# A unit's outputs copied by VectorE instead of ScalarE, with 28 score tiles moved from the attention loop to the stage before it

## The chip, the cores and the metric

The kernel runs on one core of one Trainium2 chip. The metric is the device time of one execution in microseconds (us). The kernel before takes 1575.48 us, the median of three runs (1575.44 to 1575.68).

## The reference

The input is 2048 tokens of width 512. They are normalised once, and two branches read the result:

```python
xn = _layernorm(x, axis=-1)
# A: attention, 32 heads of width 16
qkv = (xn @ wqkv).reshape(B, S, 3, H, Dh).transpose(2, 0, 3, 1, 4)
q, k, v = qkv[0], qkv[1], qkv[2]
p = _softmax(jnp.einsum("bhqd,bhkd->bhqk", q, k) * (Dh ** -0.5), axis=-1)
s = jnp.einsum("bhqk,bhkd->bhqd", p, v).transpose(0, 2, 1, 3).reshape(B, S, D) @ wo
# B: a feed-forward of width 1376, and a gate
g = _silu(_gelu(xn @ w1 + b1) @ w2 + b2)
return x + s * g
```

The softmax needs the largest score of each query row before any exponential of that row. The kernel computes every score twice: once only to find the row maxima, and once more, with keys and queries exchanged, to take the exponentials.

## The kernel before

**Units.** The 32 heads are eight groups of four, and the 2048 queries are four chunks of 512. A unit is one group with one chunk: 32 units, numbered u = 4 * group + chunk. A unit has three kinds of work.

- *Score tiles* (`s_mm`, line 171, and `s_max`, line 181). TensorE multiplies 128 queries with 512 keys of one head into one PSUM bank, and VectorE reduces the bank to two maxima a row. A unit has 64 of them, the kernel 2048. The contraction has 48 rows, so two tiles can work side by side on the two halves of TensorE's rows. When the 64th is reduced, `s_end0` (line 234) makes one further reduction of all maxima (line 239), GpSimd (POOL) splits the result into a rounded part and a rest, and `s_end1` (line 256) transposes it and sends it to DRAM, from where it comes back as two more rows of the query tile.
- *Exponential tiles* (`t_one`, line 703). TensorE multiplies 128 keys with 512 queries of one head, two more rows subtracting the maximum, and ScalarE takes the exponential (line 712). A unit has 64.
- *Output steps* (`pv_step`, line 769). Four heads' exponentials of 128 keys are multiplied with the values into one PSUM bank, `pv` (line 775), 16 times a unit. After the 16th, the bank is copied to SBUF (`os`, line 782), and transfers move the copy on (`o_move`, line 792). The pool of `pv` has one buffer, so the next unit's first output matmul waits for that copy.

**The early stage** normalises, projects, and does the feed-forward; its matmuls use one half of TensorE's rows each, in turn (`mm`, line 554, on line 561). Into this stream `fill` (line 538) puts score tiles: a slot is one matmul on each half, and a tile is due after each `ROWS / (4 * LEAD)` slots, alternately on the two halves. `ROWS` is 12 * 80 + 6 * 88 - 10 + 2 * LEAD - 38, with `LEAD` = 144 it is 1728 for 576 tiles. The tiles use two PSUM banks in turn.

**The attention loop** (line 955) has 16 steps a unit, n = 0 to 512. An order of operations is written out for each step: T is an exponential tile, S a score tile on one half, X and Y the two half-width pieces of one more tile, one on each half, and V the output step of the step before. `due(n)` (line 911) says how many score tiles shall be done by step n, and the difference chooses the order: three tiles (`TSXTTSTYV`) until step 491, none (`TTTTV`) after. Score tiles here use three PSUM banks in rotation; X keeps its bank until Y is done. A unit's output copy belongs to the V of step 16 (u + 1). From step 492 on, the first rows of the final product with `wo` fill the place of the score tiles (`w_half`, line 871).

**Key tiles.** The keys of a group lie in one of three places, group modulo three (`KB`, line 42): `kt0`, `kt1`, and two slots of the pool `big`. Groups 3 and later are loaded by POOL's DMA queue into the place of the group three before: group 3 in two halves from step 56 and step 64 (lines 916 to 919), group 4 from step 134, 5 from 198, 6 from 262, 7 from 326. Every twelfth unit takes its tiles in another order, so that a half-loaded key tile can be used (`at_of`, line 167).

What sets the order: each engine works through its instructions in the order of the program; waits between engines are derived from the tiles.

Of the kernel before, what the change touches and what calls it, by code (L numbers as in the profile page):

```python
# [8 lines left out]
F32 = mybir.dt.float32  # L9
F32R = mybir.dt.float32r  # L10
AF = mybir.ActivationFunctionType
# [5 lines left out]
P = 128  # L17
S = 2048
D = 512
H = 32  # L20
DH = 16
KT = D // P
NT = S // P
CH = 512
NCH = S // CH
# [4 lines left out]
EPS = 1e-5  # L30
SCALE = DH ** -0.5
VW = DH + 1
LEAD = 144
NW = 10
EARLY = 4
DONE = 492
FILL0 = 38
HB = 4
W2B = 2
ORDER = {0: "TTTTV", 3: "TSXTTSTYV"}  # L40
HC = CH // 2
KB = 3
XB = 6
BANKS = ("ttvt", "xtmt", "ttvt")

# [2 lines left out]
def fused(ctx: ExitStack, tc: tile.TileContext, x, wqk, wv, wo, w1, b1, w2, b2, out):  # L48
    nc = tc.nc
# [20 lines left out]
    kts, kws, qts, qzs = [], [], [], []  # L70
# [26 lines left out]
    def rows(src, g, which, a, c0, n):  # L97
        r0 = g * P + 64 * which + DH * a
        return src[r0:r0 + 48, c0:c0 + n].rearrange("(p d) s -> d p s", d=DH)[:, 0:3:2, :]

    def load_k(g, pieces=range(6), eng=nc.sync, c0=0, n=S):
        both = kws[g % KB]
        for i in pieces:
            a, b = divmod(i, 3)
            r, cs = slice(64 * a + DH * b, 64 * a + DH * b + DH), slice(c0, c0 + n)
            src = rows((qk_h, qk_h, qk_l)[b], g, 1, a, c0, n)
            if both is not None:
                eng.dma_start(both[r, :, cs].bitcast(F32), src)
            else:
                for p in range(2):  # L110
                    eng.dma_start(kts[g % KB][p][r, cs].bitcast(F32), src[:, p])

    def k_ones(kt):
        for p in range(2):
# [3 lines left out]
    def new_k(pool):  # L118
        both = pool.tile([P, 2, S], F32R, name=f"kt{len(kts)}")
        kws.append(both)  # L120
        kts.append([both[:, p] for p in range(2)])
# [3 lines left out]
    def slot(i, shape, dtype=F32):  # L125
        return big.tile(list(shape), dtype, name=f"slot{i}")

    def q_rows(qs, u, sides=range(2)):
        g, c = divmod(u, NCH)
        for a in sides:  # L130
            for b, src in enumerate((qk_h, qk_l, qk_h)):
                r = 64 * a + DH * b
                nc.sync.dma_start(qs[r:r + DH].bitcast(F32), rows(src, g, 0, a, c * CH, CH))

    def load_qs(u, sides=range(2)):
        if u < NU:
            QS[u] = qzs[u % 2] if u < LEAD // 16 else qss[0][:, u % 2]
            q_rows(QS[u], u, sides)
# [8 lines left out]
    def load_mh(u):  # L147
        assert u in sent
        for a in range(2):
            nc.sync.dma_start(QT[u][64 * a + 48:64 * a + 50].bitcast(F32), mh_d[u, :, a::2, :])  # L150
# [15 lines left out]

    def at_of(job):
        u, st, p = job
        return divmod(st, NCH) if u % (NCH * KB) else divmod(st, NCH)[::-1]

    def s_mm(ps, job, a, c0, k0, w):
        u, st, p = job
        qi, ki = at_of(job)
        if u not in MX:
            MX[u] = qring.tile([P, GH, NCH, NCH, 2], F32, name="mx")
        r = slice(64 * a, 64 * a + 3 * DH)
        k0 += ki * CH
        return nc.tensor.matmul(ps[:, c0:c0 + w], QS[u][r, p, qi * P:(qi + 1) * P],  # L178
                                kts[u // NCH % KB][p][r, k0:k0 + w], start=True, stop=True).ins

    def s_max(ps, job, heads, parts):
        u, p = job[0], job[2]
# [103 lines left out]
    for i in range(nu):  # L286
        pairs.append(ms[2 * i:2 * i + 2])
        if (i + 1) * len(qs) // nu > i * len(qs) // nu:
            g, c = qs[i * len(qs) // nu]
# [4 lines left out]
    for j in range(len(pairs)):  # L294
        for h in range(2):
# [9 lines left out]
            n = 2 if nd < len(parts) and parts[nd][2] and ready - nd > room else 1  # L305
            n = max(n, need - 2 * (left - 1))
            while nd < ready and n > 0:
                c, f, k = parts[nd]
# [33 lines left out]
    keep_v = ctx.enter_context(tc.tile_pool(name="keep_v", bufs=1, side="right"))  # L342
# [170 lines left out]
    keep_r = ctx.enter_context(tc.tile_pool(name="keep_r", bufs=1, side="right"))  # L513
# [21 lines left out]
    ndown = sum(1 for e in plan if e[0] == "down")  # L535
    ROWS = 12 * (4 * VQ + 2 * len(pairs)) + 6 * ndown - 10 + 2 * LEAD - FILL0

    def fill(a):
        due = FILL0 + sum(made) * ROWS // (4 * LEAD)
        if sum(made) < 4 * LEAD and row[a] >= due and (made[0] <= made[1]) == (a == 0):  # L540
            taken()
            if later and later[0][0] <= 0:
                s_end1(later.pop(0)[1])
            s_one(a)
            row[a] += 1
            tick()

    def taken():
        prog["pe"] += 1
        s_when.append(prog["pe"])  # L550
        if len(s_when) > 2:
            prog["seen"] = max(prog["seen"], s_when[-3])
# [142 lines left out]
    def t_tile():  # L695
        turns[0] += 1
        if turns[0] < 5:
            pool = (ps_m, ps_x, ps_a, ps_b)[turns[0] - 1]
        else:
            pool = ps_m if turns[0] % 4 == 1 else ps_t  # L700
        return pool.tile([P, CH], F32, name="pst" if pool is ps_t else "ps")

    def t_one(u, k, p, a):
        g = u // NCH
        if (u, k) not in PT:
            PT[u, k] = slot(3 + len(PN) % 3, (P, GH, CH))
            PN.append(1)
        ps = t_tile()
        r = slice(64 * a, 64 * a + 3 * DH + 2)
        nc.tensor.matmul(ps, kts[g % KB][p][r, k * P:(k + 1) * P],  # L710
                         QT[u][r, p, :], start=True, stop=True)
        nc.scalar.activation(PT[u, k][:, 2 * p + a, :], ps, AF.Exp, scale=SCALE)  # L712

# [33 lines left out]
    kp = ctx.enter_context(tc.tile_pool(name="kp", bufs=1))  # L747
# [2 lines left out]
    qts.append(kp.tile([P, 2, CH], F32R, name="qt1"))  # L750
    load_qt(1)
    load_mh(1)
    wo_h = kp.tile([P, KT, D], F32R, name="wo_h")
    wo_l = kp.tile([P, KT, D], F32R, name="wo_l")

    WR = {}

# [10 lines left out]
    PV, OS, DN, DR = {}, {}, {}, {}  # L768
    def pv_step(u, k):
        g = u // NCH  # L770
        if k == 0:
            PV[u] = ps_v.tile([P, CH], F32, name="pv")
        for j in range(GH):
            h, w = (g * GH + j) * VW, VW if k else 32
            nc.tensor.matmul(PV[u][32 * j:32 * j + w, :], vsb[:, k, h:h + w], PT[u, k][:, j, :],  # L775
                             start=(k == 0), stop=(k == NT - 1))
        del PT[u, k]
        if k == NT - 1:
            OS[u] = wb.tile([P, CH], F32, name="os", bufs=1)
            pv = PV.pop(u)  # L780
            if u < NU - 1:
                nc.scalar.activation(OS[u], pv, AF.Copy)
            else:
                nc.scalar.activation(OS[u][:, :HC], pv[:, :HC], AF.Copy)
                nc.vector.tensor_copy(OS[u][:, HC:], pv[:, HC:])
# [28 lines left out]
    GX, OTS, PW, homes = {}, {}, {}, {}  # L814

    def home(i):
        if i not in homes:
            homes[i] = (slot(i, (P, KT, D)) if i < KB else
                        keep_r.tile([P, 2 * KT, D], F32, name="kt0"))
        return homes[i]  # L820

    def load_gx(t):
        i = 2 * (t % NCH)
        if t < NW and i < 6:
            GX[t] = wb.tile([P, 2, D], F32, name="gx", bufs=3)
        elif t < NT - NCH:
            GX[t] = home(KB)[:, i - 6 * (t < NW):][:, :2]
        else:
            GX[t] = home(1 + i // KT)[:, i % KT:i % KT + 2]
        nc.sync.dma_start(GX[t][:, 0], g_d[t * P:(t + 1) * P, :])  # L830
        nc.sync.dma_start(GX[t][:, 1], x[t * P:(t + 1) * P, :])
# [73 lines left out]
    def at(n, f, *a, pos=3):  # L905
        todo.setdefault((n, pos), []).append((f, a))

    KS = tuple(range(KT))
    L = 16 * NU

    def due(n):
        return min(4 * L, 4 * LEAD + max(0, 3 * n - 1))

    for u in range(NU):
        g, c = divmod(u, NCH)
        if c == 0 and g == KB:
            for i in range(6):
                at(56 + i, load_k, g, (i,), nc.gpsimd, 0, S // 2)
                at(64 + i, load_k, g, (i,), nc.gpsimd, S // 2, S // 2)
        elif c == 0 and g > KB:  # L920
            for i in range(6):
                at(64 * (g - KB + 1) + 6 + i, load_k, g, (i,), nc.gpsimd)
        if u >= 2:
            at(16 * u - 14, load_qt, u)
            need = min(n for n in range(L) if due(n) >= 64 * (u + 1)) + (4 if u < NU - 1 else 2)
            at(max(16 * u - 14, need), load_mh, u)
        if u < NU - 1:
            at(16 * u + 17, o_move, u, pos=0)
            at(16 * u + (25 if u < NU - 2 else 19), o_den, u, pos=0)
            at(16 * u + (31 if u < NU - 2 else 22), o_div, u, nc.gpsimd)  # L930
    T3 = range(NT - NCH, NT)
    late = range(NW, NT)
    for t in range(0, NW, 2):
        n = DONE + 2 * t
# [9 lines left out]
    for i, t in enumerate(late):  # L944
        n = L - 2 * len(late) - 1 + 2 * i
# [2 lines left out]
    for i, t in enumerate(late[:2]):  # L948
        at(L - 2 + i, w_token, t)
    for k in range(KT):  # L950
        at(104 + 16 * k, load_wo, k)
        at(110 + 16 * k, wo_high, k)
        at(114 + 16 * k, wo_low, k)
    jobs.extend(heads[made[0]:])
    for n in range(L + 1):
        ua, ka = divmod(n, 16)
        want = due(n) - due(n - 1)
        i = 0
        for op in ORDER[want] if n > 1 else ("TTTTV", "TTSTSVT")[n]:
            if op in "SXY":  # L960
# [69 lines left out]
```

## Time and profile before

| | us |
|---|---|
| median of three runs | 1575.48 |
| the profiled execution | 1575.59 |
| its span, first to last instruction | 1573.8 |
| from the first score tile to the first output step | 61.4 to 477.3 |
| a unit in the loop | 32.9 |
| last output step | 1549.9 |

TensorE's granted clock is 0.999. In the rows of the profile PE is a TensorE matmul, PEld a TensorE weight load, DVE VectorE, ACT ScalarE, POOL GpSimd and SP the queue that issues most transfers; L775 is line 775. A row of the time line is: start, duration, engine, line, operation, output<-inputs, shapes, count, and in brackets the idle time of the engine before it and what ended that. Weight loads and matmuls overlap, and matmuls overlap one another.

### The profile page before, as it was taken

The numbers are of one execution on the slowest core, as the hardware profiler recorded it, in microseconds if no ns is written. First come the engines' busy times: TensorE is split into PE (matmuls) and PEld (weight loads), VectorE is DVE, ScalarE is ACT, GpSimd is POOL, SyncE is SP. The second block draws the span as 40 slices with busy tenths as digits, with TensorE's granted clock in tenths as the row PEclk, the third lists the DMA queues.
The fourth block names the chain that finished last, engine by engine and source line by source line (L and its number), as shares of the span: only waits on it lengthen the run. The fifth ranks groups of instructions, "written<-read, shape, count | busy, mean of one in ns | idle before, by whom it ended". The sixth has DMA issues, their size and how long they took to land.

```text
span 1573.8 us, 32597 instructions
## 1 busy us (share of the span) xinstructions
PE 1561.6 (99%) x12234; PEld 955.1 (61%) x12234; DVE 1376.2 (87%) x2275; ACT 1254.8 (80%) x2516; POOL 378.0 (24%) x398
## 2 busy tenths in 40 slices
PE   8999999999999999999999999999999999999998
PEld 7899999999995444444444444444444444444455
DVE  7499999999998999999999999999999999999733
ACT  4333433434339999999999999999999999999994
POOL 4135575765641001001100200000010000000144
PEclk9999999999999999999999999999999999999999
DMA  6625442454422114111511411221041111111162
GB/s 208 152 60 141 130 139 99 134 155 123 132 84 76 43 30 72 30 36 36 86 31 31 69 37 36 52 51 29 23 79 30 33 29 31 41 29 23 45 210 100
DMA packets 79486, 116.92 MB, mean 74 GB/s; under 512 B 28868, under 2 KB 29124, under 8 KB 78152
## 3 DMA queue, kind: packets, MB, share of 16 engines
q1 hardware_dynamic: 75580, 101.90, 23.9%
q0 software_dynamic: 3264, 12.35, 4.1%
q8 instruction: 96, 1.57, 0.4%
q10 hardware_dynamic: 484, 0.60, 0.1%
q14 instruction: 62, 0.51, 0.1%
HBM read 84.35 MB, written 25.97 MB: 70 GB/s over the span
## 4 chain that ended last, share of the span: by engine, by line
PE 98%; DVE 1%; issue 0%; DMA 0%; ACT 0%; POOL 0%; DVEq 0%
PE pv L775 33%; PE pst L710 16%; PE ps L710 14%; PE ps L561 13%; PE ps L178 9%; PE pst L561 7%; PE pv L561 2%; PE ps L881 1%; PE ps L438 1%; PE ps L79 1%; PE pst L79 1%; DVE st L399 0%; PE pst L422 0%; DMA xt<-in_x 0%; PE pst L438 0%
## 5 line engine op out<-in xcount | busy, mean ns | idle before, releaser
L184 DVE TENSOR_REDUCE mx<-ps 128x2 f32<-128x512 f32 x2048 | 1299.2, 685 | 129.8 <-PE ps L178 46.7
L712 ACT ACTIVATE slot<-pst 128x512 f32<-128x512 f32 x1533 | 809.5, 616 | 2.1 <-PE ps L710 0.8
L775 PE MATMUL pv<-slot,vsb 128*17 128x512 f32 (+1 forms) x4096 | 539.2, 599 | 0.0
L178 PE MATMUL ps<-kt,slot 48*128 48x512 f32 x1364 | 383.8, 370 | 1.1 <-POOLq L216 1.1
L712 ACT ACTIVATE slot<-ps 128x512 f32<-128x512 f32 x515 | 311.7, 606 | 5.6 <-PE ps L710 3.6
L710 PE MATMUL pst<-qt,kt 50*128 50x512 f32 x1149 | 311.4, 406 | 0.5 <-DVE gt L643 0.3
L710 PEld LDWEIGHTS ps<-qt,kt 50*128 50x128 f32 x387 | 70.7, 183 | 323.6 <-ACT slot L712 322.7
L710 PEld LDWEIGHTS pst<-qt,kt 50*128 50x128 f32 x1149 | 212.1, 185 | 29.7 <-ACT slot L712 11.0
L178 PEld LDWEIGHTS ps<-kt,slot 48*128 48x128 f32 x1364 | 225.4, 184 | 3.1 <-POOLq L216 1.4
L561 PE MATMUL ps<-slot,w1h 64*128 64x512 f32 x1088 | 217.7, 394 | 0.0
L178 PE MATMUL ps<-kt,qz 48*128 48x512 f32 x512 | 213.0, 416 | 0.0
L710 PE MATMUL ps<-qt,kt 50*128 50x512 f32 x387 | 190.8, 495 | 0.0
L178 PE MATMUL ps<-slot,slot 48*128 48x512 f32 x598 | 167.9, 369 | 0.0
L561 PEld LDWEIGHTS ps<-slot,w1h 64*128 64x128 f32 x1088 | 150.4, 186 | 8.6 <-ACT junk L575 2.7
L561 PE MATMUL ps<-slot,w1l 64*128 64x512 f32 x544 | 141.2, 392 | 0.0
L358 POOL TENSOR_TENSOR hl<-hg,hh 128x512 fp32r<-128x512 f32 x76 | 96.8, 1296 | 135.6 <-ACT hh L357 67.2
L575 ACT ACTIVATE junk<-ident_r 1x1 f32<-1x1 f32 x92 | 18.0, 196 | 126.7 <-PE pst L561 118.5
L775 PEld LDWEIGHTS pv<-slot,vsb 128*17 128x17 f32 (+1 forms) x4096 | 69.1, 96 | 81.7 <-issue 23.9
L178 PEld LDWEIGHTS ps<-kt,qz 48*128 48x128 f32 x512 | 93.9, 183 | 16.0 <-DVE mx L184 0.6
L710 PE MATMUL pst<-qt,slot 50*128 50x512 f32 x384 | 102.4, 407 | 0.0
L178 PEld LDWEIGHTS ps<-slot,slot 48*128 48x128 f32 x598 | 98.9, 184 | 0.9
L242 POOL CAST nmh<-nm 128x16 fp32r<-128x16 f32 x32 | 6.3, 197 | 353.6 <-PE pst L710 176.4
(151 smaller groups left out, 1756.7 us busy)
## 6 DMA issues: line engine op xcount, KB each, us to landing
raw<-in_w SPq DMA_DIRECT2D x88, 256.0 KB
qk_h<-hh SPq DMA_DIRECT2D x32, 256.0 KB
qk_l<-hl SPq DMA_DIRECT2D x32, 256.0 KB
qt<-qk_h SPq DMA_DIRECT2D x128, 64.0 KB
slot<-qk_h SPq DMA_DIRECT2D x92, 64.0 KB
g_d<-gt POOLq DMA_DIRECT2D x16, 256.0 KB, 3.3
qt<-qk_l SPq DMA_DIRECT2D x64, 64.0 KB
dn<-den_d SPq DMA_DIRECT2D x128, 32.0 KB
```

The source lines that it names most:

```text
L79: nc.tensor.matmul(ps, lhs[a], rhs[b], start=first and n == 0, stop=last and n == 2)
L178: return nc.tensor.matmul(ps[:, c0:c0 + w], QS[u][r, p, qi * P:(qi + 1) * P], kts[u // NCH % KB][p][r, k0:k0 + w], start=True, stop=True).ins
L184: nc.vector.tensor_reduce(MX[u][:, 2 * p:2 * p + 2, qi, ki][:, heads, parts], ps.rearrange("p (n c) -> p n c", c=HC), axis=AX.X, op=OP.max)
L242: nc.gpsimd.tensor_copy(hl[:, 0], nm)
L358: nc.gpsimd.tensor_sub(hl, raw, hh.bitcast(F32))
L438: nc.tensor.matmul(pq["q", g, c], W1[g][i][:, k * P:(k + 1) * P], (xh, xl)[j][c][:, k], start=n == 0 and k == 0, stop=n == 2 and k == KT - 1)
L561: i = nc.tensor.matmul(ps, lhs[r], rhs[r], start=first, stop=last).ins
L575: i = nc.scalar.activation(junk[:, :1], ident_r[:1, :1].bitcast(F32), AF.Copy).ins
L710: nc.tensor.matmul(ps, kts[g % KB][p][r, k * P:(k + 1) * P], QT[u][r, p, :], start=True, stop=True)
L712: nc.scalar.activation(PT[u, k][:, 2 * p + a, :], ps, AF.Exp, scale=SCALE)
L775: nc.tensor.matmul(PV[u][32 * j:32 * j + w, :], vsb[:, k, h:h + w], PT[u, k][:, j, :], start=(k == 0), stop=(k == NT - 1))
L881: op = nc.tensor.matmul(PW[b][0], OTS[b, k][i][r], (wo_h, wo_l)[j][r, k], start=part == 0 and n == 0, stop=part == 3 and n == 5).ins
```

## The change

1. The copy of a unit's outputs from PSUM (line 782) is made by VectorE instead of ScalarE. The last unit's, which was split between both, stays as it was.
2. `LEAD` is 151: 604 score tiles are made in the early stage, and `ROWS` becomes 1742.
3. `due` gives one tile less from step 50 on and once more every 16 steps, to step 482: those 28 steps have two score tiles and the order `TSTTSTV`. Each is the second step behind the one with a copy. Score tiles still end at step 491.
4. The fourth group (group 3) has its own key tile in the pool `kp`, where `wo_h` and `wo_l` were; these two now use the same tile later. Which group uses which place is written in `KSET`, and the step at which its load begins in `KAT`. Group 3 is loaded whole from step 4, group 4 from step 70, the others as before. The rows of ones of the new tile are written at step 3. Loading and splitting `wo` moves from step 104 to step 266. Only unit 0 takes its tiles in the other order.
5. The late gate tiles that lay in `kt0` lie in `kt1`.

```diff
-LEAD = 144
+LEAD = 151
...
-ORDER = {0: "TTTTV", 3: "TSXTTSTYV"}
+ORDER = {0: "TTTTV", 2: "TSTTSTV", 3: "TSXTTSTYV"}
+LIGHT = 34
 HC = CH // 2
-KB = 3
+KSET = (0, 1, 2, 3, 0, 2, 1, 0)
+KAT = {3: 4, 4: 70, 5: 198, 6: 262, 7: 326}
...
-        return divmod(st, NCH) if u % (NCH * KB) else divmod(st, NCH)[::-1]
+        return divmod(st, NCH) if u else divmod(st, NCH)[::-1]
...
-    wo_h = kp.tile([P, KT, D], F32R, name="wo_h")
-    wo_l = kp.tile([P, KT, D], F32R, name="wo_l")
+    new_k(kp)
+    wo_h, wo_l = [kws[3][:, i].rearrange("p (k d) -> p k d", d=D) for i in range(2)]
...
             if u < NU - 1:
-                nc.scalar.activation(OS[u], pv, AF.Copy)
+                nc.vector.tensor_copy(OS[u], pv)
...
-            homes[i] = (slot(i, (P, KT, D)) if i < KB else
-                        keep_r.tile([P, 2 * KT, D], F32, name="kt0"))
+            homes[i] = (slot(i, (P, KT, D)) if i < 3 else
+                        keep_v.tile([P, 2 * KT, D], F32, name="kt1"))
...
     def due(n):
-        return min(4 * L, 4 * LEAD + max(0, 3 * n - 1))
+        return min(4 * L, 4 * LEAD + max(0, 3 * n - 1 - max(0, (n - LIGHT) // 16)))
...
-        if c == 0 and g == KB:
+        if c == 0 and g in KAT:
+            if g == 3:
+                at(KAT[g] - 1, k_ones, kts[KSET[g]])
             for i in range(6):
-                at(56 + i, load_k, g, (i,), nc.gpsimd, 0, S // 2)
-                at(64 + i, load_k, g, (i,), nc.gpsimd, S // 2, S // 2)
-        elif c == 0 and g > KB:
-            for i in range(6):
-                at(64 * (g - KB + 1) + 6 + i, load_k, g, (i,), nc.gpsimd)
+                at(KAT[g] + i, load_k, g, (i,), nc.gpsimd)
...
-        at(104 + 16 * k, load_wo, k)
-        at(110 + 16 * k, wo_high, k)
-        at(114 + 16 * k, wo_low, k)
+        at(266 + 16 * k, load_wo, k)
+        at(272 + 16 * k, wo_high, k)
+        at(276 + 16 * k, wo_low, k)
```

Wherever a key tile was chosen by `g % KB`, it is now chosen by `KSET[g]`.

More of the change, by code (lines that the diff above doesn't have):

```diff
@@ L101, in load_k @@
     def load_k(g, pieces=range(6), eng=nc.sync, c0=0, n=S):
-        both = kws[g % KB]
+        both = kws[KSET[g]]
         for i in pieces:
@@ L110, in load_k @@
                 for p in range(2):
-                    eng.dma_start(kts[g % KB][p][r, cs].bitcast(F32), src[:, p])
+                    eng.dma_start(kts[KSET[g]][p][r, cs].bitcast(F32), src[:, p])
     def k_ones(kt):
@@ L178, in s_mm @@
         return nc.tensor.matmul(ps[:, c0:c0 + w], QS[u][r, p, qi * P:(qi + 1) * P],
-                                kts[u // NCH % KB][p][r, k0:k0 + w], start=True, stop=True).ins
+                                kts[KSET[u // NCH]][p][r, k0:k0 + w], start=True, stop=True).ins
     def s_max(ps, job, heads, parts):
@@ L709, in t_one @@
         r = slice(64 * a, 64 * a + 3 * DH + 2)
-        nc.tensor.matmul(ps, kts[g % KB][p][r, k * P:(k + 1) * P],
+        nc.tensor.matmul(ps, kts[KSET[g]][p][r, k * P:(k + 1) * P],
                          QT[u][r, p, :], start=True, stop=True)
@@ L826, in load_gx @@
         elif t < NT - NCH:
-            GX[t] = home(KB)[:, i - 6 * (t < NW):][:, :2]
+            GX[t] = home(3)[:, i - 6 * (t < NW):][:, :2]
         else:
```

## The prediction

> **What bounds the kernel now.** The page first, its chain of the work that ended last:
>
> ```profile
> PE 98%; DVE 1%; issue 0%; DMA 0%; ACT 0%; POOL 0%; DVEq 0%
> ```
>
> TensorE (PE) carries 98% of it, which names the engine and not the waits. So I cut the span by stage (PE, PEld, DVE, ACT, POOL busy):
>
> ```profile
> 62.00:477.00 415.00, 414.62 (x3481) 379.80 (x3479) 375.13 (x598) 159.43 (x357) 238.78 (x210) 1.00 0.42 121
> 478.00:1472.00 994.00, 993.89 (x7723) 473.95 (x7720) 921.75 (x1523) 991.18 (x1960) 75.57 (x126) 1.00 0.19 41
> 1472.00:1549.00 77.00, 75.92 (x597) 38.83 (x595) 33.97 (x52) 72.16 (x139) 28.46 (x23) 1.00 0.45 145
> ```
>
> The early stage is TensorE's, with 40 us of VectorE free. The loop has TensorE and ScalarE both full. The chain gives a unit's length, and the time line one end of a unit (start, duration):
>
> ```profile
> 873.00 1.07 PE pv L775 x8
> ...
> 905.91 1.07 PE pv L775 x8
> ```
> ```profile
> 870.90 1.05 PE L775 MATMUL pv<-slot,vsb 128*17 128x512 f32 x8
> ...
> 873.00 0.16 PEld L775 LDWEIGHTS pv<-slot,vsb 128*32 128x32 f32 x8 [0.21 <-ACT os L782]
> ...
> 874.96 0.18 PEld L710 LDWEIGHTS pst<-qt,kt 50*128 50x128 f32 x1 [0.30 <-ACT slot L712]
> ...
> 875.39 1.05 PE L775 MATMUL pv<-slot,vsb 128*17 128x512 f32 x8
> ...
> 877.41 1.05 PE L775 MATMUL pv<-slot,vsb 128*17 128x512 f32 x8
> ```
>
> A unit takes 905.91 - 873.00 = 32.91 us. Its ordinary step is 2.02 to 2.03 (875.39 to 877.41; I use 2.03); the two steps at its end take 2.10 (870.90 to 873.00) and 2.39 (873.00 to 875.39). So a unit holds 0.07 + 0.36 = 0.43 us that come from one thing: ScalarE's copy of the outputs pushes its exponentials back, and weights wait for them.
>
> **The change, part by part.**
>
> *The copy leaves ScalarE.* It goes in 31 units. The last of these copies lies among the steps after 1472, where no score tiles are left and VectorE works 34 of 77 us; it is worth nothing there. 30 x 0.43 = **-12.9 us**.
>
> *The copy on VectorE.* These rows show its queue, and what its lateness would meet:
>
> ```profile
> 871.03 1.28 DVE L184 TENSOR_REDUCE mx<-ps 128x2 f32<-128x512 f32 x2
> ```
> ```profile
> 870.89 1.57 ACT L712 ACTIVATE slot<-pst 128x512 f32<-128x512 f32 x3
> ...
> 872.45 0.41 PE L178 MATMUL ps<-kt,slot 48*128 48x512 f32 x1
> ...
> 872.57 0.43 PE L710 MATMUL pst<-qt,kt 50*128 50x512 f32 x1
> ...
> 876.94 1.89 DVE L184 TENSOR_REDUCE mx<-ps 128x2 f32<-128x512 f32 x3 [0.29 <-PE ps L178]
> ```
>
> Maxima of 0.68 start (1.89 - 0.68) / 2 = 0.60 apart, three a step, 1.81 of 2.03. The step's last maximum starts at 871.63 and ends at 872.31; the copy starts 0.60 behind it, at 872.23, and takes 0.69 if it is like a maximum (no row shows it whole; the nearest reads the same 128x512 from PSUM). It ends at 872.92. The next unit's first output matmul, due at 872.93, waits some 0.04 for it: 30 x 0.04 = **+1.3** (nothing if it is shorter, 3 if 0.1 late).
>
> Behind it the next step's maxima come 0.39 late (872.84 instead of 872.45). The bank of a step's third tile is wanted 0.57 into the next step (the matmul at 872.45; steps begin at 869.86, as a row below shows, and 2.03 later) and is now free at 0.43. Late by 0.39, it would stall that step by 0.25 and some weight loading, 0.3. The step of two score tiles stands there: it does not ask for that bank, and VectorE skips 0.60 of work. So it costs nothing in 28 units; units 0 and 1 have no such step: **+0.6**.
>
> *Light steps.* 28 tiles leave the loop. Each was two half-width matmuls side by side on the two row halves, about 0.12 us. A fourth exponential ends at 870.89 + 1.57 = 872.46, its bank's next matmul starts at 872.57: only 0.11 to spare. Of 0.12, I count 0.08: 28 x 0.08 = **-2.2** (0 to -3.4).
>
> *The unit's closing reduction moves.*
>
> ```profile
> 566.07 1.05 PE L775 MATMUL pv<-slot,vsb 128*17 128x512 f32 x8
> 566.18 0.28 DVE L239 TENSOR_REDUCE nm<-mx 128x16 f32<-128x128 f32 x1
> ...
> 568.26 1.05 PE L775 MATMUL pv<-slot,vsb 128*17 128x512 f32 x8
> ```
>
> Where it falls behind a step's first maximum, it adds 0.2 to VectorE, the third bank comes 0.11 late, and the step takes 2.19: 0.16 lost. That is so in 7 units now and, by the changed order, 13 times: **+1.0**.
>
> *28 more tiles in the early stage.* Each of the rows below is a score tile's matmul or weights (PE, PEld) or its maximum (DVE):
>
> ```profile
> 320.03 0.43 PE L178 MATMUL ps<-kt,qz 48*128 48x512 f32 x1
> ...
> 321.37 0.18 PEld L178 LDWEIGHTS ps<-kt,qz 48*128 48x128 f32 x1
> ...
> 321.47 0.41 PE L178 MATMUL ps<-kt,qz 48*128 48x512 f32 x1
> ...
> 322.21 0.18 PEld L178 LDWEIGHTS ps<-kt,qz 48*128 48x128 f32 x1
> ```
> ```profile
> 320.64 0.68 DVE L184 TENSOR_REDUCE mx<-ps 128x2 f32<-128x512 f32 x1
> ```
> ```profile
> 321.47 0.69 DVE L184 TENSOR_REDUCE mx<-ps 128x2 f32<-128x512 f32 x1
> ```
>
> Two tiles of one bank lie 1728 x 2 / 576 = 6 slots apart (a slot is one matmul on each row half): 320.03 to 321.47, 0.24 a slot. 28 tiles are 14 slots on each half: **+3.4** if nothing waits.
>
> But maxima end at 321.32 and 322.16, and the weights of the tile two behind load at 321.37 and 322.21: 0.05 later both times. They wait for VectorE, and that is hidden only because the matmul starts 0.10 after its weights (321.47). The new spacing is 1742 / 604 = 2.884 slots, which means that 604 x 3 - 1742 = 70 of the spacings are two slots instead of three. Each puts two tiles of one bank 5 slots, 1.20 us, apart. The shortest bank cycle follows from a tile that met an idle array and an idle VectorE:
>
> ```profile
> 869.86 0.50 PE L178 MATMUL ps<-kt,slot 48*128 48x512 f32 x1
> ```
> ```profile
> 870.43 0.69 DVE L184 TENSOR_REDUCE mx<-ps 128x2 f32<-128x512 f32 x1
> ```
>
> 0.57 + 0.69 + 0.05 = 1.31: the bank comes 0.11 late. Bounds: 0 (the matmuls queued on the other half cover it) and 0.24 (the removed slot is lost whole). The nearest row is the step of 2.19 above, where a bank 0.11 late cost 0.16: I take 0.15. 70 x 0.15 = **+10.5**.
>
> The Trainium skill, "TensorEngine Tiling (Array Packing)", section "PSUM Bottleneck", says that tiling speeds up TensorE but not the emptying of PSUM, which may become the limit. The trace agrees (the 0.05 above); if emptying were the whole limit, 28 tiles would cost their full 0.72 each, the second rival's case.
>
> *The fourth group's own key tile.* Its score tiles now begin at step 55, while group 0 is used up to step 64, so it needs a place of its own. Loaded at steps 4 to 9 on POOL's queue, four one-rows at step 3 on SP's, 45 steps (90 us) ahead of use: nothing. Were that place not free, the reductions' rounding on POOL and the query loads on SP would queue behind it; they have most of a unit to spare. The loads of wo move to step 266 and are used at 492: nothing.
>
> **Sum.** -12.9 + 1.3 + 0.6 - 2.2 + 1.0 = -12.2 in the loop, 3.4 + 10.5 = +13.9 before it: **+1.7**. The profiled execution took 1575.6 (1.8 around the span), the median 1575.5: I forecast **1577.2**, no change that can be told. It turns at 70 x = 8.8, that is at 0.126 per short spacing.
>
> **Rivals.**
> 1. *The short spacings are covered* (0.04 each or less). For it: the weights are asked for early, and VectorE idles 40 us there. Against: no lead is left but 0.10. Early stage +6.2: 1569.5. Faster.
> 2. *The early stage runs at VectorE's pace*: a short spacing costs the whole slot, 0.24, beyond the 0.126 at which the sign turns. For it: every weight load quoted waits. Against: the chain's own 1.31 is below 6 slots. 3.4 + 16.8 = 20.2 early: 1583.5. Slower.
> 3. *The light step does not catch the copy*: 0.3 more in 28 units, 8.4: 1585.6. Against: 0.60 of relief for 0.39 of lateness.
> 4. *The long steps are the unit's turn, not the copy*: the -12.9 and the 1.3 fall away, 1588.8. Against: both waits name ScalarE.
> 5. *VectorE overlaps nothing*: three maxima of 0.685 fill 2.06, the loop becomes VectorE's, and with 47 of them, the copy and 0.6 of small work a unit takes 33.5: 28 x (33.5 - 32.9) + 13.9, some 1606. The Trainium skill has this as a rule ("VectorE: DVE Perf Modes", "The DRAIN you can't avoid": the next operation waits for an empty pipe). The 0.60 between starts speaks against it.
>
> **How the numbers follow.** Forecast 0.40 (0.10 to 0.18 a spacing, own range 1573 to 1580), rival 1 0.30, rival 2 0.18, rival 3 0.06, rival 4 0.05, rival 5 0.01. A measurement of this kernel tells about 0.2%, 3.15 us, from no change. Faster: 0.27 of rival 1. Same: 0.33 of the forecast and 0.03 of rival 1. Slower: 0.07 of the forecast and rivals 2 to 5, 0.37 together. For 8 in 10 the range reaches from rival 1's times, with the light steps at their best, to rival 2's: 1567 to 1584.
>
> **What would show it.** Right: steps at a unit's end of 2.03 to 2.08, units of 32.4 to 32.5, light steps under 2.0, an early stage 14 us longer with score weights waiting at the short spacings. Wrong: an early stage only 3 to 6 us longer (rival 1) or 20 (rival 2); the third step behind a unit's end above 2.1 (rival 3); long steps that stay (rival 4).

## The result, and the profile after

The changed kernel takes **1585.18 us** (median; 1584.85 to 1585.45), the kernel before in the same runs 1575.58: a ratio of 1.0058 (95% interval 1.0046 to 1.0070). It is slower by 9.6 us; the forecast was 1577.2 with a range up to 1584.0. The profiled spans are 1583.1 and 1573.8, 9.3 apart. One execution of a run below (a tile for each part of the copy) took 2064.74 us at a granted clock of 0.655 and is left out of that run's time.

Three dates divide these 9.3 us: the first step of outputs, the last one, and the end. These are the time lines of before and then of after (start, duration, engine, line; the second row of each holds the last two steps, the first of which starts at the time shown; the last one starts at 1549.89 and 1559.34):

```profile
477.27 1.07 PE L775 MATMUL pv<-slot,vsb 128*32 128x512 f32 x8
...
1549.01 1.91 PE L775 MATMUL pv<-slot,vsb 128*17 128x512 f32 x16
```
```profile
495.92 1.07 PE L777 MATMUL pv<-slot,vsb 128*32 128x512 f32 x8
...
1558.47 1.91 PE L777 MATMUL pv<-slot,vsb 128*17 128x512 f32 x16
```

The early stage ends 495.92 - 477.27 = **18.65 us later** (forecast 13.9), the loop takes 1063.42 instead of 1072.62, **9.2 less** (forecast 12.2 less), and what follows takes nearly the same, 23.7 and 23.9. (The changed kernel's lines stand two lower: outputs L777, score matmuls L180, maxima L186, the matmuls of the exponential tiles L712, exponentials L714, copy L784.)

After by stages (PE, PEld, DVE, ACT and POOL busy with their instructions, granted clock, DMA share, GB/s):

```profile
62.00:495.50 433.50, 433.10 (x3509) 385.05 (x3506) 393.00 (x628) 159.06 (x357) 239.07 (x212) 1.00 0.41 117
497.00:1480.00 983.00, 982.74 (x7653) 468.07 (x7657) 915.41 (x1521) 979.14 (x1927) 71.87 (x117) 1.00 0.20 41
1480.00:1558.00 78.00, 76.92 (x606) 39.30 (x600) 35.47 (x55) 72.77 (x140) 28.43 (x23) 1.00 0.45 147
```

Nothing here looks worse than before: TensorE is as full, VectorE as far from full in the early stage (393 of 433.5; 375 of 415 before). The difference shows only when one counts what the time produced. The maxima of a stretch of 360 us in the middle of the early stage, before and then after:

```profile
100.00:460.00 360.00, 325.02 (x505) 1.00 0.44 129
```
```profile
100.00:460.00 360.00, 325.84 (x506) 1.00 0.43 123
```

505 tiles against 506. TensorE's own count in that stretch, before and then after, fell, though it counts as busy for all of it:

```profile
100.00:460.00 360.00, 360.00 (x3026) 1.00 0.44 129
```
```profile
100.00:460.00 360.00, 360.00 (x2919) 1.00 0.43 123
```

The change asks for a tile every 2.884 slots instead of 3.00, and gets them at the old pace, 360 / 506 = 0.711 us each; so 28 more of them are 28 x 0.711 = 19.9 us more (1.3 of it comes back: from the first early maximum to the last, a tile takes 0.7123 instead of 0.7145). In the loop, a unit's end shows the other half of the result (outputs of TensorE, then VectorE, then ScalarE, of after):

```profile
886.58 1.05 PE L777 MATMUL pv<-slot,vsb 128*17 128x512 f32 x8
...
888.64 1.06 PE L777 MATMUL pv<-slot,vsb 128*32 128x512 f32 x8
...
890.64 1.05 PE L777 MATMUL pv<-slot,vsb 128*17 128x512 f32 x8
...
892.72 1.05 PE L777 MATMUL pv<-slot,vsb 128*17 128x512 f32 x8
...
894.74 1.05 PE L777 MATMUL pv<-slot,vsb 128*17 128x512 f32 x8
```
```profile
887.90 0.68 DVE L784 COPY os<-pv 128x512 f32<-128x512 f32 x1
888.50 3.07 DVE L186 TENSOR_REDUCE mx<-ps 128x2 f32<-128x512 f32 x5
892.19 1.89 DVE L186 TENSOR_REDUCE mx<-ps 128x2 f32<-128x512 f32 x3 [0.62 <-PE ps L180]
```
```profile
890.17 0.60 ACT L714 ACTIVATE slot<-ps 128x512 f32<-128x512 f32 x1
...
890.66 1.57 ACT L714 ACTIVATE slot<-pst 128x512 f32<-128x512 f32 x3
...
892.15 0.60 ACT L714 ACTIVATE slot<-ps 128x512 f32<-128x512 f32 x1
```

The step of 2.39 is gone. The copy takes 0.68, the next maximum starts 0.60 behind it, and the five maxima of the next step and the light step follow without a gap; VectorE is then idle for 0.62, so it has caught up, as the forecast said. But the light step takes 2.00 (888.64 to 890.64) and the step behind it 2.08: together 4.08, no less than two ordinary steps. Its left-out tile brought nothing. ScalarE's exponentials (the last rows) follow each other without idle time there, four from 890.17 to 892.15.

### The profile page after: what moved, and what is told of

Same layout as the page of the kernel before. It is cut to its first block, busy times and chain, and to the rows that moved or that the text cites. A ratio compares the mean times of both kernels' runs of the same rounds, so it can differ in the third digit from the quotient of the medians.

```text
span 1583.1 us, 32472 instructions
## 1 busy us (share of the span) xinstructions
PE 1571.0 (99%) x12206; PEld 955.5 (60%) x12206; DVE 1389.6 (88%) x2306; ACT 1243.6 (79%) x2485; POOL 374.9 (24%) x392
## 3 DMA queue, kind: packets, MB, share of 16 engines
q1 hardware_dynamic: 75596, 101.96, 23.9%
## 4 chain that ended last, share of the span: by engine, by line
PE 98%; DVE 1%; DMA 0%; issue 0%; ACT 0%; POOL 0%; DVEq 0%
PE pv L777 32%; PE pst L712 15%; PE ps L712 14%; PE ps L563 13%; PE ps L180 11%; PE pst L563 7%; PE pv L563 2%; PE ps L883 1%; PE ps L440 1%; PE ps L81 1%; PE pst L81 1%; DVE st L401 0%; PE pst L424 0%; DMA xt<-in_x 0%; PE pst L440 0%; DVE slot L76 0%
## 5 line engine op out<-in xcount | busy, mean ns | idle before, releaser
L186 DVE TENSOR_REDUCE mx<-ps 128x2 f32<-128x512 f32 x2048 | 1297.6, 685 | 125.9 <-PE ps L180 50.0
L714 ACT ACTIVATE slot<-pst 128x512 f32<-128x512 f32 x1533 | 804.2, 605 | 2.2 <-PE ps L712 0.8
L777 PE MATMUL pv<-slot,vsb 128*17 128x512 f32 (+1 forms) x4096 | 539.1, 598 | 0.2 <-DVE os L784 0.2
L180 PE MATMUL ps<-kt,slot 48*128 48x512 f32 x1350 | 382.9, 371 | 1.1 <-POOLq L218 1.1
L714 ACT ACTIVATE slot<-ps 128x512 f32<-128x512 f32 x515 | 307.3, 597 | 7.3 <-PE ps L712 3.9
L712 PE MATMUL pst<-qt,kt 50*128 50x512 f32 x1149 | 304.4, 405 | 0.5 <-DVE gt L645 0.3
L712 PEld LDWEIGHTS ps<-qt,kt 50*128 50x128 f32 x387 | 70.6, 183 | 323.8 <-ACT slot L714 322.9
L563 PE MATMUL ps<-slot,w1h 64*128 64x512 f32 x1088 | 227.3, 394 | 0.0
L180 PEld LDWEIGHTS ps<-kt,slot 48*128 48x128 f32 x1350 | 223.1, 184 | 5.7 <-POOLq L218 1.4
L180 PE MATMUL ps<-kt,qz 48*128 48x512 f32 x512 | 222.6, 435 | 0.0
L712 PEld LDWEIGHTS pst<-qt,kt 50*128 50x128 f32 x1149 | 207.5, 185 | 22.0 <-DVE gt L645 1.2
L712 PE MATMUL ps<-qt,kt 50*128 50x512 f32 x387 | 190.7, 495 | 0.0
L180 PE MATMUL ps<-slot,slot 48*128 48x512 f32 x584 | 169.0, 373 | 0.0
L563 PEld LDWEIGHTS ps<-slot,w1h 64*128 64x128 f32 x1088 | 155.2, 185 | 8.1 <-ACT junk L577 1.9
L563 PE MATMUL ps<-slot,w1l 64*128 64x512 f32 x544 | 147.8, 393 | 0.0
L777 PEld LDWEIGHTS pv<-slot,vsb 128*17 128x17 f32 (+1 forms) x4096 | 68.8, 96 | 83.2 <-issue 29.9
L180 PEld LDWEIGHTS ps<-kt,qz 48*128 48x128 f32 x512 | 93.7, 183 | 25.4 <-DVE mx L186 9.4
L712 PE MATMUL pst<-qt,slot 50*128 50x512 f32 x384 | 99.7, 405 | 0.0
L180 PEld LDWEIGHTS ps<-slot,slot 48*128 48x128 f32 x584 | 97.0, 184 | 3.3 <-DVE mx L186 1.0
L814 POOL TENSOR_TENSOR slot<-slot,dn 64x512 f32<-64x512 f32 x16 | 20.5, 1280 | 312.7 <-PE pst L712 175.0
```

The lines of the kernel that those rows point to most:

```text
L186: nc.vector.tensor_reduce(MX[u][:, 2 * p:2 * p + 2, qi, ki][:, heads, parts], ps.rearrange("p (n c) -> p n c", c=HC), axis=AX.X, op=OP.max)
L563: i = nc.tensor.matmul(ps, lhs[r], rhs[r], start=first, stop=last).ins
L712: nc.tensor.matmul(ps, kts[KSET[g]][p][r, k * P:(k + 1) * P], QT[u][r, p, :], start=True, stop=True)
L814: eng.tensor_mul(ot[c][rs, g // 2], ot[c][rs, g // 2], DN.pop(u)[rs])
```

## The experiments

Each kernel was timed in three rounds beside the kernel before on the same chip; the ratio is to before (1575.3 to 1575.7 in these runs).

### The copy alone

```diff
 before
-                nc.scalar.activation(OS[u], pv, AF.Copy)
+                nc.vector.tensor_copy(OS[u], pv)
```

> The kernel before with the copy alone moved to VectorE: 576 early tiles, no light steps, old key tiles. Theory (the early stage pays for the tiles, the loop gains from the copy): the early stage stays at 415 us; of the 0.43 us a unit that ScalarE's copy cost, 0.38 go, and the third bank that comes late costs about 0.31 in each of 30 units (the changed kernel shows steps of 2.34 where no light step follows): 1575.5 - 12.9 + 1.3 + 9.3 = 1573. Rival (the light steps made the gain in the loop, VectorE falls behind for several steps without them): no gain or a loss, 1576 to 1584.

Measured: **1573.24 us**, ratio 0.9985 (0.9976 to 0.9994). Its outputs at a unit's end:

```profile
870.13 1.05 PE L775 MATMUL pv<-slot,vsb 128*17 128x512 f32 x8
...
872.19 1.07 PE L775 MATMUL pv<-slot,vsb 128*32 128x512 f32 x8
...
874.52 1.05 PE L775 MATMUL pv<-slot,vsb 128*17 128x512 f32 x8
...
876.55 1.05 PE L775 MATMUL pv<-slot,vsb 128*17 128x512 f32 x8
```

The two steps take 2.06 and 2.33 instead of 2.10 and 2.39. VectorE's lateness costs 0.30 without a light step, the 0.3 that the forecast put on units 0 and 1, and leaves 0.10 a unit of what the change of engine brings: 2.5 us less in the loop. Of all versions that leave nothing out, this one takes the least time.

### The change with ScalarE's copy

```diff
 after
-                nc.vector.tensor_copy(OS[u], pv)
+                nc.scalar.activation(OS[u], pv, AF.Copy)
```

> The changed kernel with the copy back on ScalarE, all else kept. Theory: the early stage stays 18.7 us longer than before, the loop loses the copy's 12 us again and keeps what the light steps are worth by themselves (0 to 3 us): 1594 to 1597, steps behind a unit's end of 2.39 again. Rival (the light step takes up ScalarE's delay as it takes up VectorE's): about 1588.

Measured: **1595.02 us**, ratio 1.0123 (1.0106 to 1.0139). The steps of 2.39 are back:

```profile
889.93 1.05 PE L777 MATMUL pv<-slot,vsb 128*17 128x512 f32 x8
...
892.02 1.07 PE L777 MATMUL pv<-slot,vsb 128*32 128x512 f32 x8
...
894.41 1.05 PE L777 MATMUL pv<-slot,vsb 128*17 128x512 f32 x8
```

So the long steps are the copy, not the unit's turn (rival 4 is out). The loop takes 0.9 us *more* than before, with 28 light steps in it: steps of 2.12 to 2.27 number 13 instead of 7, as forecast for the closing reduction (6 x 0.16 = 1.0), and the light steps, which are the very steps of 2.39 here, bring nothing.

### Closer tiles, and no more of them

```diff
 before
-    ROWS = ... + 2 * LEAD - FILL0
+    ROWS = ... + 2 * LEAD - FILL0 - 70
```

> The kernel before with its 576 early tiles put closer, 1658 / 576 = 2.878 slots apart instead of 3, so that 70 spacings are two slots; the last 70 slots of the stage then hold no tile. No matmul is added. Theory (a bank's cycle through VectorE sets the pace, 0.7 us a tile): each short spacing costs 0.2 to 0.24, the stage gets 14 to 17 us longer, 1590 to 1592. Rival (the 28 added tiles themselves or what else moved cost the time, the queue covers a short spacing): 1575 to 1578.

Measured: **1596.63 us**, ratio 1.0131 (1.0116 to 1.0146): the theory's direction, and beyond its size. Its count of maxima, and its last early one (before's last three start at 471.24 and follow each other):

```profile
100.00:460.00 360.00, 325.87 (x506) 1.00 0.43 123
```
```profile
471.58 0.69 DVE L184 TENSOR_REDUCE mx<-ps 128x2 f32<-128x512 f32 x1
494.38 0.14 DVE L573 COPY junk<-ident_r 1x1 f32<-1x1 f32 x1 [22.10 <-PE pv L561]
```

The tiles were asked for 4% closer and came at the old pace, 506 in 360 us. The 70 slots stand behind the last tile instead, where no tile shares them: the loop begins at 498.53, 21.3 later, 0.30 a slot. That is more than a slot. TensorE there waits twice for ScalarE, which the kernel before doesn't show, and runs at a lower clock behind the first wait:

```profile
480.61 0.51 PE L561 MATMUL pst<-w2h,hh 64*128 64x512 f32 x2 [1.83 <-ACT junk L575]
...
492.62 0.49 PE L561 MATMUL pst<-w2h,hh 64*128 64x512 f32 x2 [1.65 <-ACT junk L575]
```
```profile
480.50:485.00 4.50, 4.39 (x24) 3.55 (x26) 0.00 (x0) 0.06 (x1) 2.05 (x2) 0.62 0.00 0
485.00:490.00 5.00, 5.00 (x44) 3.94 (x44) 0.00 (x0) 0.72 (x2) 1.29 (x1) 1.00 0.01 3
```

### A few closer tiles

```diff
 before
-    ROWS = ... + 2 * LEAD - FILL0
+    ROWS = ... + 2 * LEAD - FILL0 - 20
```

> The kernel before with its 576 early tiles asked for in 20 slots less, so that 20 spacings, one in 29, are two slots instead of three. Theory: the tiles of one pair of banks can't come faster than 0.712 to 0.714 us each, however few of the spacings are short; the last tile comes when it did, and the 20 slots follow it: 20 x 0.234 to 0.30 = 4.7 to 6.0 more, 1580.2 to 1581.6. Rival: a single short spacing is covered by the long ones around it and costs 0.1 or less, and 70 of them were costly because they lie close together: 1575.5 to 1577.5.

Measured: **1580.82 us**, ratio 1.0036 (1.0022 to 1.0051), 5.5 more for 20 slots (0.28 each).

```profile
100.00:460.00 360.00, 325.97 (x507) 1.00 0.44 128
```

A single short spacing among 28 long ones isn't covered either. No spacing under three slots made the tiles come faster: 505, 507, 506 and 506 in 360 us, for 3.00, 2.965, 2.884 and 2.878 slots.

### Shorter maxima in the early stage

The change, with the early maxima over half of the columns (the rest of those columns is left out; the softmax of these units is softened so that nothing overflows).

```diff
 after
+        src = ps.rearrange("p (n c) -> p n c", c=HC)
+        if "seen" in prog:
+            src = src[:, :, :HC // 2]
-        nc.vector.tensor_reduce(MX[u]..., ps.rearrange("p (n c) -> p n c", c=HC), ...)
+        nc.vector.tensor_reduce(MX[u]..., src, ...)
```

> The changed kernel with the early maxima taken over the first half of each 256 columns only (it leaves out half of the scores there, and softens the exponentials of the first ten units so that they stay finite). Theory (VectorE's maximum is the long part of a bank's cycle): the cycle falls from 1.31 us to about 1.05, below 5 slots, the short spacings cost nothing, the early stage is 3 to 4 us longer than before instead of 18.7: 1569 to 1571. Rival (TensorE pays for the tiles in another way): stays at 1583 to 1585.

Measured: **1562.01 us**, ratio 0.9913 (0.9899 to 0.9928), 7 less than the least that was expected.

```profile
100.00:460.00 360.00, 224.15 (x534) 1.00 0.46 130
```

Now the spacing asked for is the spacing that comes: 360 / 534 = 0.674 us, which is 2.884 slots of 0.234. The stage ends at 473.02, 22.9 earlier than in the change, and 4.3 earlier than in the kernel *before*, with 28 more tiles; it had been expected 3 to 4 later than there. What held the tiles is the maximum, and it held the kernel before too, by 4.3 + 3.4 = some 7.7 us.

### Early tiles that begin sooner

With the split copy of the run below, so that its 1581.27 is the measure here.

```diff
 split copy (below)
-FILL0 = 38
+FILL0 = 24
```

> The split copy of the run beside it, and the early score tiles begin 14 slots sooner (FILL0 24 instead of 38), so that their spacing grows from 3.00 to 3.02 slots. Theory: the early tiles of the kernel before already run at the two banks' pace of 0.7145 us a tile and not at three slots of 0.234 = 0.702, so that the stage ends 14 x 0.234 = 3.3 sooner when they begin 3.3 sooner: 3 to 3.5 less than the run beside it, with the same 0.714 a tile. Rival A: the stage's length is TensorE's slots, and the same number of slots takes the same time: no difference (under 0.8). Rival B: the first tiles meet keys or queries that are not yet there, and TensorE stands in front of them: equal or longer, with a wait for a DMA at 58 us.

Measured: **1580.63 us**, 0.6 less than the 1581.27: rival A's result.

```profile
100.00:460.00 360.00, 323.67 (x502) 1.00 0.44 129
```

The tiles begin 3.1 earlier and end 1.0 earlier, at 0.718 us each. So the pace of before isn't one fixed 0.7145: above three slots tiles come as they are asked for, with some waiting left in the slots (0.718 / 3.024 = 0.2375, against 0.234 in the run with shorter maxima). Where those last 0.004 a slot are lost stays open.

### Light steps apart from the copy

```diff
 after
-LIGHT = 34
+LIGHT = 40
```

> The changed kernel with the 28 steps of two score tiles moved half a unit away from the copy (LIGHT 40 instead of 34: step 8 of a unit instead of step 2). Theory: the light step's only use is to take up VectorE's 0.4 us of lateness behind the copy; without it the second step behind each unit's end is 2.34 as in units 1 and 2, 28 x 0.31 = 8.7 more, and the light steps in their new place still save nothing (2.00 or longer): 1594 us (1592 to 1596), with 28 steps above 2.25. Rival A: a light step that is not used up by the copy saves its two half-width matmuls, 0.1 each: the same 8.7, less 28 x 0.1: 1591. Rival B: VectorE's lateness needs no light step, units 1 and 2 are slow for being the first: 1585, no steps above 2.25.

Measured: **1592.5 us**, ratio 1.0109 (1.0094 to 1.0124), between the theory's 1594 and rival A's 1591, by the time alone. The steps decide; a unit's end, and the light step half a unit later:

```profile
891.21 1.06 PE L777 MATMUL pv<-slot,vsb 128*32 128x512 f32 x8
...
893.54 1.05 PE L777 MATMUL pv<-slot,vsb 128*17 128x512 f32 x8
...
903.68 1.05 PE L777 MATMUL pv<-slot,vsb 128*17 128x512 f32 x8
...
905.71 1.05 PE L777 MATMUL pv<-slot,vsb 128*17 128x512 f32 x8
```

The step behind a unit's end takes 2.33 to 2.34 again (2.53 once), and the light step takes 2.03 to 2.05 in 27 of 28 units (1.88 in the other), as its neighbours do. So a light step has one use here: VectorE's lateness. There it is worth something, since the loop takes 1063.42 in the changed kernel and 1070.10 with the copy alone; but these 6.7 us were paid for with 18.65 in the early stage.

### Exponentials narrowed around the light step

The change, with the exponentials of steps 1 to 5 of each unit over half of their columns (ones stand in the other half).

```diff
 after
+            if 1 <= k <= 5:
+                nc.gpsimd.memset(PT[u, k][:, :, HC:], 1.0)
-        nc.scalar.activation(PT[u, k][:, 2 * p + a, :], ps, AF.Exp, scale=SCALE)
+        w = HC if 1 <= k <= 5 else CH
+        nc.scalar.activation(PT[u, k][:, 2 * p + a, :w], ps[:, :w], AF.Exp, scale=SCALE)
```

> The changed kernel with the exponentials of steps 1 to 5 of every unit over 256 of 512 columns (the other half of the exponentials is left out there; GpSimd writes ones in its place), which relieves ScalarE around the light step (step 2). Theory: a light step saved nothing because ScalarE's four exponentials fill it as they fill any other step; with ScalarE relieved the light step is 0.08 to 0.15 shorter than the steps of three tiles beside it (3 to 5), which fall to 1.80 to 1.95 themselves: 1555 us (1545 to 1570). Rival: TensorE gains nothing from the left-out tile, because its half-width matmul runs beside another: the light step stays within 0.04 of the steps of three tiles beside it.

Measured: **1582.76 us**, ratio 1.0047 (1.0032 to 1.0062), 28 more than expected. The same unit's end:

```profile
886.24 1.05 PE L780 MATMUL pv<-slot,vsb 128*17 128x512 f32 x8
...
888.30 1.07 PE L780 MATMUL pv<-slot,vsb 128*32 128x512 f32 x8
...
890.20 1.05 PE L780 MATMUL pv<-slot,vsb 128*17 128x512 f32 x8
...
892.21 1.05 PE L780 MATMUL pv<-slot,vsb 128*17 128x512 f32 x8
...
894.23 1.05 PE L780 MATMUL pv<-slot,vsb 128*17 128x512 f32 x8
```

The light step takes 1.90, the steps of three tiles beside it 2.01 and 2.02: with ScalarE relieved, a left-out tile is worth 0.12, the very number that the forecast had for its matmuls. That half of the theory holds. The other half fails: the steps of three tiles did not fall to 1.80 to 1.95. They take 2.02 with ScalarE idle in part. So a step is filled twice: without ScalarE's limit it takes 2.02 for three tiles and 1.90 for two, and ScalarE's four exponentials need some 2.0 in either.

### The copy cut in two

Every unit's copy as the last unit has it in the kernel before.

```diff
 before
-            if u < NU - 1:
-                nc.scalar.activation(OS[u], pv, AF.Copy)
-            else:
-                nc.scalar.activation(OS[u][:, :HC], pv[:, :HC], AF.Copy)
-                nc.vector.tensor_copy(OS[u][:, HC:], pv[:, HC:])
+            nc.scalar.activation(OS[u][:, :HC], pv[:, :HC], AF.Copy)
+            nc.vector.tensor_copy(OS[u][:, HC:], pv[:, HC:])
```

> The kernel before with every unit's copy cut in two by columns, the first 256 on ScalarE and the last 256 on VectorE, as it does for its last unit now; no light steps, 576 early tiles. Theory: ScalarE is pushed back by half a copy (about 0.25 of the 0.48) and VectorE by about 0.35, which the slack of 0.11 to 0.14 of either ring partly takes up: the 0.43 a unit falls to 0.10 to 0.25, 30 x 0.18 to 0.33 less, 1568 us (1565 to 1571). Rival: the fixed part of a copy dominates, half a copy costs as much as a whole one on each engine, and the unit loses on both: 1573 to 1578.

Measured: **1581.27 us**, ratio 1.0037 (1.0024 to 1.0050), slower than before, where 1568 was expected.

```profile
907.64 0.42 ACT L781 ACTIVATE os<-pv 128x256 f32<-128x256 f32 x1
...
908.09 0.42 DVE L782 COPY os<-pv 128x256 f32<-128x256 f32 x1 [0.45 <-ACT os L781]
908.43 1.88 DVE L184 TENSOR_REDUCE mx<-ps 128x2 f32<-128x512 f32 x3
...
908.57 1.06 PE L775 MATMUL pv<-slot,vsb 128*32 128x512 f32 x8 [0.23 <-DVE os L782]
```

The halves are short, 0.42 each, but VectorE's waits 0.45 for ScalarE's. So both engines come late, and the outputs' bank comes free late as well: the two steps take 2.33 and 2.34.

### The same with a tile for each part

```diff
 split copy
+                OS[u] = [wb.tile([P, w], F32, name=f"os{i}", bufs=1) for i, w in enumerate((AC, CH - AC))]
+                nc.scalar.activation(OS[u][0], pv[:, :AC], AF.Copy)
+                nc.vector.tensor_copy(OS[u][1], pv[:, AC:])
```

with AC = 256 and then 128 columns; the moves and the reading of the denominators are cut at the same column, and the last unit is left as it was.

> The split copy again, with a tile of its own for each half (and the moves behind it cut in two), in the kernel before; the last unit is left as it is. In the first split VectorE's half started 0.03 us after ScalarE's half had ended, 0.45 after VectorE was free, so that the outputs' bank came free late and both engines were late. Theory: that order came from the shared output tile; with two tiles the halves run side by side, 0.42 each, the next unit's outputs don't wait, ScalarE is pushed back by 0.26 and VectorE by 0.34, and a unit loses 0.10 to 0.25 instead of 0.43: 1568 us (1565 to 1571). Rival: two engines don't read one bank of PSUM at a time, VectorE's half still starts behind ScalarE's: 1580 to 1583.

> As the run beside it, with 128 of the 512 columns on ScalarE and 384 on VectorE. If the halves run side by side: ScalarE is pushed back by about 0.15, which its slack of 0.11 nearly takes up, and VectorE by about 0.47, somewhat more than the 0.14 to 0.29 that the score banks' ring can take; a unit loses 0.15 to 0.30: 1568 to 1573, between the run beside it and the copy on VectorE alone (1573.2). If the parts run one behind the other: 1580 to 1583.

Measured: **1589.82 us**, ratio 1.0091 (1.0074 to 1.0108), and **1589.90 us**, ratio 1.0092 (1.0075 to 1.0109), beyond what either expectation had.

```profile
908.71 0.41 ACT L783 ACTIVATE os<-pv 128x256 f32<-128x256 f32 x1
...
909.15 0.42 DVE L784 COPY os<-pv 128x256 f32<-128x256 f32 x1 [0.45 <-ACT os L783]
```

The 0.45 stays (2.34 and 2.33, and with the quarter 2.37 and 2.34), so the shared output tile was not its cause. What the parts still share is the bank that they read; that it is the cause was not tested. The Trainium skill, "PSUM — Partial Sum Buffer", section "PSUM bank collisions raise a hardware error", says that two engines which access one bank and the same partitions at once, even two reads, collide, and that a scheduler therefore puts such accesses in order; the 0.45 agrees with that, but no run here shows what would happen without the wait. The loop is 7.3 us longer than in the first split. Of these, 5.4 lie in the last unit, where two steps take 7.1 and 4.4 (7.4 and 4.0 with the quarter) instead of 3.05; the additional moves are the likely cause, which was not followed further.

### The key tile and the loads alone

```diff
 after
-LEAD = 151
+LEAD = 144
-        return min(4 * L, 4 * LEAD + max(0, 3 * n - 1 - max(0, (n - LIGHT) // 16)))
+        return min(4 * L, 4 * LEAD + max(0, 3 * n - 1))
-                nc.vector.tensor_copy(OS[u], pv)
+                nc.scalar.activation(OS[u], pv, AF.Copy)
```

> The changed kernel with only the fourth head group's own key tile, its earlier loads and the later loads of the output weights left: ScalarE copies the outputs, no light steps, 576 early tiles. Theory: these moves cost nothing, 1575.5 us (1574.5 to 1577). Rival: they cost part of what the change lost in the loop, through POOL's or SP's queue, up to 2 or 3 us: 1577.5 to 1579, with longer steps in the first units (steps 4 to 9 and 266 to 280).

Measured: **1575.27 us**, ratio 1.0000 (0.9991 to 1.0010). The moves of the keys and of wo cost nothing, as forecast.

## Why the prediction was wrong, point by point

The time came out 8.0 us above the forecast; 4.75 of these are the early stage's (18.65 for 13.9) and 3.0 the loop's (-9.2 for -12.2). Neither alone would have carried it out of the range.

**The step that failed is the early stage's price**, "70 x 0.15 = +10.5". Rival 2's mechanism came true: a tile costs what the two banks' round trip takes, not the slots that it fills, and a short spacing loses nearly the whole slot (rival 1 is out). Measured, 18.65 - 3.4 = 15.25 us are lost in 70 short spacings, 0.22 each, and 0.28 to 0.30 in the two runs that shortened the spacing alone. Rival 2 had 20.2 early and 1583.5 in all; with its light steps at nothing instead of 2.2 that is 1585.7, and 1585.2 was measured. That they agree so closely is partly luck: its early stage was 1.5 too long, its loop 0.8 too short. The range ended at 1584.0 because rival 2's time kept the likeliest value of another uncertain term.

Two readings went wrong on the way to 0.15.

*The slot.* The forecast took 0.24 us for a slot from two tiles of one bank that lie 6 slots apart (320.03 to 321.47). Ahead of the first tile, the kernel before shows slots without any:

```profile
58.16 0.39 PE L561 MATMUL pv<-kt,slot 64*128 64x512 f32 x1
...
60.45 0.39 PE L561 MATMUL pv<-kt,slot 64*128 64x512 f32 x1
```

Ten slots in 2.29 us: 0.229. Six are 1.37, and the pair took 1.44. The 0.24 already held waiting, so the forecast measured a queue with a ruler that the queue had stretched. Against slots of 0.229 to 0.234, three to a tile are 0.69 to 0.70, under the 0.7145 at which tiles came: the maxima held the tiles back before the change already. The run with shorter maxima shows it: some 7.7 us of the stage of before were VectorE's.

*The nearest row.* The 0.16 for a bank 0.11 late came from a step in the loop. It happens once there, and the steps behind it make good a lateness. In the early stage nearly every tile waits for its bank already, so nothing is made good: of the weight loads of before, 559 of 574 start 0.05 to 0.06 behind the end of the maximum that frees their bank (592 of 602 in the changed kernel, 75 of 602 with the shorter maxima).

The profile's own account of waits hid this. The weights of the early score tiles that waited for a maximum, before and then after (total, times, longest):

```profile
PEld ps L178 <- DVE mx L184: 0.6, 4, 0.2
```
```profile
PEld ps L180 <- DVE mx L186: 10.7, 38, 0.4
```

It counts a load as waiting only while PEld is idle, and PEld was busy 379.80 of 415 us there. The forecast had found the loads 0.05 behind a maximum and still priced them as covered in part.

**The copy leaves ScalarE, -12.9:** right in mechanism. Without it the 2.39 is gone, and with it the 2.39 is back. On average over the units of before, the two steps are 0.355 and 0.06 longer than an ordinary one, so the term is 30 x 0.415 = 12.5.

**The copy on VectorE, +1.3** (its 30 x 0.04 is 1.2)**:** about right. The weights of the next unit's first outputs load at 888.63, 0.05 after the copy has ended at 888.58:

```profile
888.63 0.16 PEld L777 LDWEIGHTS pv<-slot,vsb 128*32 128x32 f32 x8 [0.17 <-DVE os L784]
```

They do so in 29 of the 30 units. The unit's last step takes 2.06 on average (the long steps of the closing reduction left out), 0.03 more than an ordinary one, which makes 30 x 0.03 = 0.9. The copy's start 0.60 behind the last maximum and its 0.68 were as forecast. Units without a light step lose 0.31 (forecast 0.3), and the light step does take up the lateness in the others (rival 3 is out), though the step behind it stays 0.04 longer than an ordinary one: 28 x 0.04 = 1.1.

**Light steps, -2.2:** wrong; in themselves they are worth nothing half a unit later, and 28 x 0.036 = 1.0 where they stand, which the step behind them takes back. The matmuls saved are worth 0.12, but ScalarE's four exponentials fill a step of two tiles as they fill one of three. The prediction's own row had said so: ScalarE was busy 991.18 of 994 us in the loop. The 0.11 "to spare" was not slack that a shorter step could use.

**The closing reduction, +1.0:** right with ScalarE's copy (13 long steps); with VectorE's copy there are 17, 1.6.

Together in the loop: -12.5 + 0.9 + 0.6 + 1.1 - 1.0 + 1.6 = -9.3, and -9.2 was measured.

**The key tile and the loads, nothing:** right (1575.27 against 1575.28). **Rival 5:** out; the five maxima behind the copy start 0.60 apart at 0.68 each, so the loop isn't VectorE's.

What stays open: the 0.004 us a slot that tiles at 3.02 slots still cost, and why a run of tiles (2 x 0.712 = 1.42) never reaches the 1.31 that the forecast put together. In part it is VectorE's queue: 292 of the 603 distances between the early maxima of the changed kernel are under 0.62, the pace at which maxima follow each other without a gap, and a maximum starts 0.60 behind its matmul at the median, against 0.47 with the shorter maxima.

## What to carry to other kernels

Before work is moved into a stage, count what that stage delivers in a fixed time (tiles in 360 us here) and compare it with what its slots would allow where nothing waits; if the two differ, something other than the full engine sets the pace, and each moved piece costs that pace. A gain on one engine is only worth as much as the second engine leaves: where ScalarE is busy 991 of 994 us, matmuls saved on TensorE shorten nothing. An engine that takes over work pays also for the lateness that it passes on through its ring of banks, 0.30 a unit here, and splitting such a copy over two engines didn't help, because the second part waited for the first.

## What the runs showed of the hardware

- Two engines' copies of different columns of one bank ran one behind the other, with a wait of 0.45 us, whether they wrote one tile or two; two short copies on two engines cost more (1581.3) than one long copy on either (1573.2 and 1575.5).
- A wait of TensorE of 1.83 us was followed by a lower granted clock: 0.62 on average over the next 4.5 us, 1.00 after it (the rows above). Behind the wait of 1.65 us, 12 us later in the same run, the clock stayed at 1.00. The Trainium skill, "TensorE: Matmul & The Clock Gate", section "What's actually happening", tells of half the clock after an idle window of about 3.4 us; here the wait was shorter than that.
- VectorE's maxima and its copy, 0.68 each from PSUM, start 0.60 apart when they queue up, six in a row (887.90 to 891.57).
